# Expert slots of an attention-and-experts kernel: weight planes issued in another order, conversions after the relu, token counts in registers

## Chip, cores and metric

One core of one Trainium2 chip. The metric is the device time of one execution in microseconds (us), the median of the runs shown; smaller is better.

## What is computed

Three layers, one after the other, on 1792 tokens of 768 numbers:

```python
attn = softmax(mask(q @ k.T / 8)) @ v             # 4 x 12 heads, 448 x 64 each
e = argmax(x @ w_gate, axis=1)                    # one of 8 experts per token
for e in range(8):
    h = np.maximum(x[mask] @ w1[e], 0.0)          # 768 -> 1024
    out[mask] = gate * eom * (h @ w2[e])          # 1024 -> 768
h = x @ w_in                                      # 768 -> 2048
y = (h - np.tanh(h)) @ w_out                      # 2048 -> 768
```

## The kernel before

Three stages stand one after the other on the matmul engine (PE): attention, the experts, and the last two matmuls. Every matmul of float32 numbers in the last two stages is made of three float16 matmuls: a number is split into a high plane (the number rounded to float16) and a low plane (the rest), and high x high, high x low and low x high are added. So every weight has to be converted: `scaled` (L110) makes the high plane on ScalarE (ACT), GpSimd (POOL) or VectorE (DVE), and `rest_of` (L118) makes the low plane on DVE or POOL from the float32 number and the high plane.

The change lies in the expert stage. Tokens are sorted by expert into blocks of 128. One block of one expert is a **slot** (`slot`, L812): the matmuls with w1 in two halves of 512 hidden numbers (`slot_mm1`, L157); after each half a relu that writes its high plane hh on ACT and its low plane hl on DVE (`slot_relu`, L164 and L165); the transposition of the token rows of the following slots on PE, copied from PSUM by ACT (high) and DVE (low) (`slot_xT`, L144 to L148); and the matmuls with w2 in two halves of 384 columns (`slot_mm2`, L169), each copied out by ACT into yo (L831) and stored by a DMA (L837).

Every expert has a **first slot**, which always runs, and up to 13 **further slots**, nested in each other, each behind a branch on the expert's token count (`extra`, L847). With these inputs the experts 0 to 7 run 0, 1, 2, 0, 1, 0, 4 and 1 further slots, so 17 slots in all. The count is loaded from SBUF into a register of every engine before each first slot (L1104).

Beside its own matmuls a slot does other work, handed to it as `fill` and called at four positions z = 0 to 3 (after each relu, after each half of w2):

- A first slot of expert e converts the weights of expert e+1 by a table (`PLAN`, L914, and `PLANS` for two experts): for each position some row blocks (0, k) of w1 and (1, k) of w2, with the engine of the high and that of the low plane. `pieces` (L130) issues the high planes of a position, its low planes, and then on the SyncE (SP) queue the loads of expert e+2's rows into the same float32 buffer (L104).
- A further slot converts units of 128 x 1024 numbers of the last stage's weights (`conv`, L876): six DVE instructions (L864, L867, L870) that make float32 of 64-bit words, two ACT instructions for the high plane and two on DVE or four on POOL for the low one. `CPE` gives one to three units per slot, by expert, and `conv_fill` (L890) their positions. Each unit is loaded (L874) and stored again (L885) by SP.

```python
        for fg in range(2):
            ph = slot_mm1(e, i, fg, w, tag)
            slot_relu(fg, ph, hh, hl)
            (fill if late else early)(fg)
```

All engines run their instructions in the order written: nothing is rescheduled. So what stands ahead of a relu on ACT or DVE holds it up, and what stands ahead of a load on SP holds that up. At a branch that is not taken SP and POOL wait for their DMAs under way before they go on (L851).

## Time and profile before

| | |
|---|---|
| device time, median of 3 runs | 1089.51 us (1086.93 to 1093.47) |
| profiled execution: its own time, its span | 1095.17 us, 1093.1 us |
| busy in the span: PE, DVE, POOL, ACT | 1000.8, 830.8, 611.3, 591.9 us |
| mean granted clock of PE | 0.98 |
| expert stage, about 264 to 613 us | 349.2 us, PE busy 302.1 |
| last stage, 613 us to the end | 479.9 us, PE busy 454.2 |

The profile lists each instruction with start and duration, and with the idle time of its engine before it and the event that ended it. An engine that is not busy costs nothing by itself; what counts is idle time of PE, which the other engines feed.

### The profile page before, as it was taken

Reading aid. Unit: us, or ns where it says so; the run is one execution under the profiler, and the core shown is the slowest. Engines: PE = TensorE matmul, PEld = TensorE weight load, DVE = VectorE, ACT = ScalarE, POOL = GpSimd, SP = SyncE. Lnnn points to the kernel's source line nnn. Section 1 sums busy time; section 2 is a strip of 40 time slices with the busy share of each in tenths; the row PEclk is TensorE's granted clock in tenths of the full one; section 3 lists DMA queues with packets and bytes.
Section 4 is the critical chain, followed back from the end, with each engine's and each line's share of the span. In section 5 each row is a group of like instructions: output and inputs, shape, how many; then the busy total and the mean of one; then the engine's idle time right before and its main releaser. Section 6 shows DMA issues by size and latency. Waiting matters only on the chain. (4 is left out here: it accounts for less than half of the span.)

```text
span 1093.1 us, 24262 instructions
## 1 busy us (share of the span) xinstructions
PE 1000.8 (92%) x9186; PEld 749.4 (69%) x9186; DVE 830.8 (76%) x1579; ACT 591.9 (54%) x1190; POOL 611.3 (56%) x623
## 2 busy tenths in 40 slices
PE   5999999998888899789898877999999999999996
PEld 4999998996657667467667544566666666667763
DVE  7778887776896767688785799998788888776640
ACT  4687866773534255263232476666565656655530
POOL 5576765684876348587325867755554444443321
PEclk9999998999999999899999999999999999999998
DMA  8899996735977968984896625010000000000000
GB/s 249 206 252 301 248 273 175 216 99 169 325 256 283 305 233 280 347 273 159 306 315 243 249 115 207 3 42 31 14 24 30 22 27 18 15 16 15 16 23 22
DMA packets 62833, 174.93 MB, mean 160 GB/s; under 512 B 8400, under 2 KB 23376, under 8 KB 59584
## 3 DMA queue, kind: packets, MB, share of 16 engines
q1 hardware_dynamic: 56352, 147.20, 41.1%
q0 software_dynamic: 6304, 25.63, 8.3%
q8 instruction: 80, 1.31, 0.5%
q14 instruction: 97, 0.79, 0.2%
HBM read 133.09 MB, written 29.62 MB: 149 GB/s over the span
## 5 line engine op out<-in xcount | busy, mean ns | idle before, releaser
L1231 PE MATMUL fo<-wo,g 128*128 128x384 f16 x1344 | 228.2, 326 | 0.0
L1180 PEld LDWEIGHTS <-raw 128*128 128x128 f16 x1440 | 141.4, 98 | 95.8 <-issue 18.2
L1231 PEld LDWEIGHTS <-g 128*128 128x128 f16 x1344 | 131.2, 98 | 83.8
L1190 POOL TENSOR_TENSOR V<-cu,cc 128x384 f32<-128x384 f32 (+1 forms) x80 | 77.0, 963 | 197.8 <-ACT cu L1189 197.7
L157 PEld LDWEIGHTS <-w 128*128 128x128 f16 x2592 | 147.8, 99 | 17.4 <-issue 16.4
L169 PE MATMUL py<-w,hh 128*128 128x384 f16 x544 | 137.2, 335 | 18.7 <-ACT hh L164 18.6
L1180 PE MATMUL fh<-cu,raw 128*128 128x384 f16 (+1 forms) x864 | 133.9, 311 | 11.7 <-DVE cc L1188 11.6
L343 ACT ACTIVATE P<-s,nb 112x112 f32<-112x112 f32 (+1 forms) x192 | 90.2, 497 | 62.0 <-DVE nb L337 36.6
L380 PE MATMUL o<-v,PT 112*112 112x65 f32 x960 | 115.9, 261 | 0.0
L120 DVE SCALAR_TENSOR_TENSOR w<-raw,w 128x768 f16<-128x768 f32 (+1 forms) x70 | 99.0, 1455 | 19.0 <-ACT w L112 16.2
L380 PEld LDWEIGHTS o<-v,PT 112*112 112x112 f32 x960 | 106.8, 180 | 0.2 <-ACT xt L402 0.2
L1208 DVE TENSOR_TENSOR V<-V,co 128x384 f32<-128x384 f32 (+1 forms) x80 | 99.9, 1249 | 0.0
L169 PE MATMUL py<-w,hl 128*128 128x384 f16 x272 | 91.1, 335 | 8.0 <-DVE hl L165 7.9
L1189 ACT ACTIVATE cu<-cc 128x384 f32<-128x384 f32 (+1 forms) x80 | 40.1, 502 | 102.5 <-DVE cc L1188 102.5
L1193 POOL TENSOR_TENSOR X<-cc,X 128x384 f32<-128x384 f32 (+1 forms) x80 | 91.0, 1138 | 4.2 <-ACT X L1192 0.5
L1188 DVE TENSOR_TENSOR cc<-fh,co 128x384 f32<-128x384 f32 (+1 forms) x80 | 42.0, 525 | 65.8 <-PE fh L1180 53.9
L169 PEld LDWEIGHTS <-hh 128*128 128x128 f16 x544 | 52.8, 100 | 54.5 <-ACT hh L164 21.9
L329 DVE TENSOR_REDUCE nm<-s 112x2 f32<-112x224 f32 (+1 forms) x144 | 77.2, 536 | 15.7 <-PE s L321 14.2
L128 POOL TENSOR_TENSOR w<-scm,w 128x512 f16<-128x512 f32 (+1 forms) x58 | 77.0, 1327 | 18.6 <-issue 10.9
L1200 DVE SCALAR_TENSOR_TENSOR V<-cu,V 128x384 f32<-128x384 f32 (+1 forms) x80 | 86.7, 1084 | 0.1
L112 ACT ACTIVATE w<-raw 128x768 f16<-128x768 f32 (+2 forms) x101 | 84.1, 892 | 0.0
L157 PE MATMUL ph<-xT_n,w 128*128 128x128 f16 x1152 | 68.4, 222 | 12.2 <-issue 3.5
(430 smaller groups left out, 2049.5 us busy)
## 6 DMA issues: line engine op xcount, KB each, us to landing
raw<-w SPq DMA_DIRECT2D x48, 512.0 KB
raw<-w SPq DMA_DIRECT2D x60, 384.0 KB
cu<-wf SPq DMA_DIRECT2D x22, 1024.0 KB
wb_d<-co SPq DMA_DIRECT2D x22, 512.0 KB
raw<-kq SPq DMA_DIRECT2D x11, 896.0 KB
ys_d<-yo SPq DMA_DIRECT2D x17, 384.0 KB
raw<-wb_d SPq DMA_DIRECT2D x8, 768.0 KB
xs_d<-xq SPq DMA_DIRECT2D x24, 224.0 KB
```

What stands on the lines that cost most here:

```text
L112: nc.scalar.activation(out=out, in_=in_, func=AF.Copy, scale=WS)
L120: nc.vector.scalar_tensor_tensor(out=out, in0=in_, scalar=WS, in1=hi, op0=ALU.mult, op1=ALU.subtract)
L157: nc.tensor.matmul(out=ph[:, (f % 4) * 128 : (f % 4 + 1) * 128], lhsT=w[0][:, ww, k, f * 128 : (f + 1) * 128], rhs=xTs[tag][:, xx, k, :], ...
L169: nc.tensor.matmul(out=py[:, 0:384], lhsT=hx[:, k, :], rhs=w[1][:, ww, k, z * 384 : (z + 1) * 384], start=(k == 0 and n == 0), stop=(k == ...
L329: nc.vector.tensor_reduce(out=nm[:, c0:c1], in_=d["s", m], op=ALU.max, axis=AX.X, negate=True)
L343: nc.scalar.activation(out=d["P"][:, j, OFF[i] : OFF[i] + n], in_=d["s", m][:, z, :], func=AF.Exp, bias=d["nb"][:, 2 * i + j : 2 * i + j + ...
L380: nc.tensor.matmul(out=po[:, i, :], lhsT=d["PT"][:, g, o : o + CP], rhs=d["t"][3][:, hl, j, :], start=(j == 0), stop=(j == i))
L1180: nc.tensor.matmul(out=ph[:, 0:nt], lhsT=wi[ww][:, f // 4, k, f % 4 * 128 : (f % 4 + 1) * 128], rhs=yy[:, k, 0:nt], start=(q == 0), stop=( ...
L1193: nc.gpsimd.tensor_tensor(out=d["X"], in0=d["h"], in1=d["X"], op=ALU.subtract)
L1200: nc.vector.scalar_tensor_tensor(out=d["V"], in0=d[f"S{z}"], scalar=QD[z - 1], in1=d["V"], op0=ALU.add, op1=ALU.mult)
L1208: nc.vector.tensor_tensor(out=d["V"], in0=d["V"], in1=G[g % 2]["rs"][:, 1, 0:nt], op=ALU.mult)
L1231: nc.tensor.matmul(out=po[:, 0:384], lhsT=t[:, x, k, i * 128 : (i + 1) * 128], rhs=wo_[ww][:, k, z * 384 : (z + 1) * 384], start=(k == 0 a ...
```

## The change

The positions of a slot are written out. High planes get five positions of their own, low planes keep four. The high planes of the first table entry are split: its first two go ahead of the w1 matmuls of the slot, the rest behind the first relu. The row transposition goes ahead of the conversions that followed the second relu. Units of the last stage's weights go to the positions 1 and 3 (two per slot) or 1, 2 and 3 (three per slot); position 0 is gone. All eight counts are loaded into registers ahead of expert 0's first slot.

```diff
     def slot(e, i, w, tag, fill=None, trans=(), then=(), late=False):
-        early = (lambda z: None) if late else fill
+        hi, lo = fill if isinstance(fill, tuple) else (lambda z: None, lambda z: None)
         fill = fill if late else (lambda z: None)
...
-        for fg in range(2):
-            ph = slot_mm1(e, i, fg, w, tag)
-            slot_relu(fg, ph, hh, hl)
-            (fill if late else early)(fg)
...
-            py = slot_mm2(e, i, z, w, hh, hl)
-            early(2 + z)
...
+        hi(0)
+        slot_relu(0, slot_mm1(e, i, 0, w, tag), hh, hl)
+        hi(1)
+        lo(0)
+        slot_relu(1, slot_mm1(e, i, 1, w, tag), hh, hl)
+        rows_T(0)
+        fill(1)
+        hi(2)
+        lo(1)
+        py = slot_mm2(e, i, 0, w, hh, hl)
+        hi(3)
+        out_z(0, py)
+        rows_T(1)
+        lo(2)
+        py = slot_mm2(e, i, 1, w, hh, hl)
+        hi(4)
+        lo(3)
+        out_z(1, py)
...
-                if z == (((1,), (0, 2), (1, 2, 3)) if i == 1 + FB[e] else ((1,), (0, 2), (0, 1, 2)))[c - 1][j]:
+                if z == ((1,), (1, 3), (1, 2, 3))[c - 1][j]:
...
+            def fill_hi(z, e=e):
+                plan = PLANS.get(e, PLAN)
+                todo = (plan[0][:2], plan[0][2:])[z] if z < 2 else plan[z - 1]
+                pieces_hi(wts[e + 1], todo)
...
-        cntr = nc.values_load(cnt[0:1, e : e + 1], min_val=0, max_val=NT)
+        if e == 0:
+            cntrs += [nc.values_load(cnt[0:1, x : x + 1], min_val=0, max_val=NT) for x in range(E)]
+        cntr = cntrs[e]
```

`rows_T(z)` is the transposition of a following slot's rows with the gather behind it; `out_z` copies a half of w2's result into yo and then calls `fill(2 + z)`; `fill_lo` calls `pieces` without its high planes.

The order on ACT in the first slot of expert 4 (w_5 are the weights of expert 5, hh the relu, xT and xT_n transposed rows, yo the result). Before:

```order
L164 ACTIVATE hh_0_21138<-ph_0_0_21141 128x512
L112 ACTIVATE w_5_21107<-raw_89 128x1024 x3
L164 ACTIVATE hh_0_21138<-ph_0_1_21228 128x512
L112 ACTIVATE w_5_21107<-raw_89 128x1024 x2
L148 ACTIVATE xT_4488<-pt_I-21315_21316 128x768
L112 ACTIVATE w_5_21108<-raw_90 128x768 x2
L831 ACTIVATE yo_0_21140<-py_0_0_21334 128x384
```

and with the change:

```order
L112 ACTIVATE w_5_21163<-raw_89 128x1024 x2
L168 ACTIVATE hh_0_21180<-ph_0_0_21185 128x512
L112 ACTIVATE w_5_21163<-raw_89 128x1024
L168 ACTIVATE hh_0_21180<-ph_0_1_21270 128x512
L152 ACTIVATE xT_4488<-pt_I-21345_21346 128x768
L112 ACTIVATE w_5_21163<-raw_89 128x1024 x2
L112 ACTIVATE w_5_21164<-raw_90 128x768 x2
L832 ACTIVATE yo_0_21182<-py_0_0_21376 128x384
```

Two high planes moved ahead of the first relu, and the copy of the transposed rows ahead of two others.

The order on DVE in the same slot (hl is the relu's low plane, w_5 low planes but for the one TENSOR_SCALAR). Before:

```order
L165 SCALAR_TENSOR_TENSOR hl_0_21139<-ph_0_0_21141,hh_0_21138 128x512
L120 SCALAR_TENSOR_TENSOR w_5_21107<-raw_89,w_5_21107 128x1024 x2
L165 SCALAR_TENSOR_TENSOR hl_0_21139<-ph_0_1_21228,hh_0_21138 128x512
L120 SCALAR_TENSOR_TENSOR w_5_21107<-raw_89,w_5_21107 128x1024 x2
L146 COPY xT_4488<-pt_I-21324_21325 128x768
L116 TENSOR_SCALAR w_5_21108<-raw_90 128x768
L120 SCALAR_TENSOR_TENSOR w_5_21108<-raw_90,w_5_21108 128x768 x2
L146 COPY xT_n_4486<-pt_I-21381_21382 128x768
L120 SCALAR_TENSOR_TENSOR w_5_21108<-raw_90,w_5_21108 128x768 x4
```

and with the change:

```order
L169 SCALAR_TENSOR_TENSOR hl_0_21181<-ph_0_0_21185,hh_0_21180 128x512
L120 SCALAR_TENSOR_TENSOR w_5_21163<-raw_89,w_5_21163 128x1024 x2
L169 SCALAR_TENSOR_TENSOR hl_0_21181<-ph_0_1_21270,hh_0_21180 128x512
L150 COPY xT_4488<-pt_I-21354_21355 128x768
L120 SCALAR_TENSOR_TENSOR w_5_21163<-raw_89,w_5_21163 128x1024 x2
L116 TENSOR_SCALAR w_5_21164<-raw_90 128x768
L150 COPY xT_n_4486<-pt_I-21414_21415 128x768
L120 SCALAR_TENSOR_TENSOR w_5_21164<-raw_90,w_5_21164 128x768 x6
```

Both copies of transposed rows moved up by two low planes each.

The order on ACT in the further slot of expert 4, with two units (co are the converted units). Before:

```order
L164 ACTIVATE hh_1_21462<-ph_1_0_21465 128x512
L112 ACTIVATE co_4888<-cc 128x512 x2
L164 ACTIVATE hh_1_21462<-ph_1_1_21572 128x512
L148 ACTIVATE xT_4487<-pt_I-21647_21648 128x768
L831 ACTIVATE yo_1_21464<-py_1_0_21666 128x384
L112 ACTIVATE co_4889<-cc 128x512 x2
L831 ACTIVATE yo_1_21464<-py_1_1_21724 128x384
```

and with the change:

```order
L168 ACTIVATE hh_1_21504<-ph_1_0_21507 128x512
L168 ACTIVATE hh_1_21504<-ph_1_1_21582 128x512
L152 ACTIVATE xT_4487<-pt_I-21657_21658 128x768
L112 ACTIVATE co_4986<-cc 128x512 x2
L832 ACTIVATE yo_1_21506<-py_1_0_21708 128x384
L832 ACTIVATE yo_1_21506<-py_1_1_21734 128x384
L112 ACTIVATE co_4987<-cc 128x512 x2
```

The first unit moved from between the relus to behind both and behind the copy of the rows; the second from ahead of the second result to behind it, where the next slot's first relu follows.

## Rows read from the trace of the kernel before

**Rows 1.** Experts, last stage: length, busy PE, PEld, DVE, ACT, POOL (us), clock, DMA share, GB/s.
```profile
264.00:613.20 349.20, 302.08 (x3571) 234.91 (x3569) 264.40 (x371) 145.39 (x221) 210.42 (x190) 0.97 0.79 275
613.20:1093.10 479.90, 454.20 (x2966) 284.72 (x2966) 366.64 (x602) 269.25 (x545) 235.90 (x224) 0.99 0.12 44
```

**Rows 2.** Waits of PE in the expert stage: us in total, times, longest.
```profile
PE py L169 <- ACT hh L164: 18.6, 9, 5.0
PE py L169 <- DVE hl L165: 7.9, 14, 1.5
...
PE pt_I-25681_25682 L144 <- DVE xT L146: 1.4, 1, 1.4
...
PE pt_I-21381_21382 L144 <- DVE xT L146: 0.6, 1, 0.6
```

**Rows 3.** PE in time, further slots: the longest waits for the second relu.
```profile
446.60 0.82 PE L169 MATMUL py<-w,hh 128*128 128x384 f16 x2 [4.98 <-ACT hh L164]
...
529.95 0.50 PE L169 MATMUL py<-w,hh 128*128 128x384 f16 x2 [4.15 <-ACT hh L164]
```

**Rows 4.** ACT in time, expert 4's further slot, at the 4.98 us wait.
```profile
443.93 0.63 ACT L112 ACTIVATE co<-cc 128x512 f16<-128x512 f32 x1 [6.68 <-DVE cc L870]
...
445.96 0.58 ACT L164 ACTIVATE hh<-ph 128x512 f16<-128x512 f32 x1
```

**Rows 5.** Stretches behind that wait: busy of five engines, granted clock, DMA share, GB/s.
```profile
446.50:449.00 2.50, 1.40 (x4) 0.42 (x5) 2.50 (x5) 0.74 (x2) 2.26 (x3) 0.50 0.89 313
449.00:452.00 3.00, 3.00 (x11) 1.46 (x10) 3.00 (x6) 0.16 (x1) 0.47 (x1) 0.50 0.98 337
```

**Rows 6.** DVE instructions on a unit: ns min/median/max, first and last start.
```profile
L870 DVE SCALAR_TENSOR_TENSOR cc<-cu,cc x44: 675/683/1640, 316.3 to 596.4; 128x512 uint32<-128x512 uint32 x44
```

**Rows 7.** DVE and SP in time: a unit's load issued, and the conversion that waited for it.
```profile
367.40 0.36 SPq L874 DMA_DIRECT2D cu<-wf  x1
...
378.33 0.76 DVE L864 TENSOR_SCALAR cc<-cu 128x512 uint32<-128x512 uint32 x2 [2.28 <-DMA cu<-wf]
```

**Rows 8.** Stretch of expert 6's second further slot, three units.
```profile
514.00:534.00 20.00, 14.87 (x181) 11.40 (x181) 17.42 (x32) 6.04 (x12) 4.87 (x5) 0.93 0.94 335
```

**Rows 9.** PE and DVE in time, expert 3's first slot: start, second transposition.
```profile
391.98 8.21 PE L157 MATMUL ph<-xT_n,w 128*128 128x128 f16 x144 [1.04 <-ACTq L851]
...
406.32 0.49 PE L144 MATMUL pt_I-17081_17082<-identh,xg_n 128*128 128x128 f16 x6 [1.23 <-DVE xT L146]
...
402.25 3.55 DVE L120 SCALAR_TENSOR_TENSOR w<-raw,w 128x1024 f16<-128x1024 f32 x2
405.72 0.55 DVE L146 COPY xT<-pt_I-17024_17025 128x768 f16<-128x768 f16 x1
```

**Rows 10.** POOL and ACT in time, first slots of experts 3 and 4.
```profile
397.93 1.16 POOL L128 TENSOR_TENSOR w<-scm,w 128x512 f16<-128x512 f32 x1 [5.02 <-issue]
...
431.53 0.49 ACT L831 ACTIVATE yo<-py 128x384 f32<-128x384 f32 x1 [6.72 <-SPq L851]
```

**Rows 11.** The loads of the counts on PE and DVE: ns min/median/max, first and last start.
```profile
L1104 PEldq TENSOR_LOAD <-cnt x8: 301/310/497, 261.6 to 574.6; - x8
...
L1104 DVEq TENSOR_LOAD <-cnt x8: 300/330/1623, 273.2 to 584.2; - x8
```

**Rows 12.** Page: low planes on DVE. Then DVE and PE in experts 0 and 1.
```profile
L120 DVE SCALAR_TENSOR_TENSOR w<-raw,w 128x768 f16<-128x768 f32 (+1 forms) x70 | 99.0, 1455 | 19.0 <-ACT w L112 16.2
...
274.16 0.69 DVE L165 SCALAR_TENSOR_TENSOR hl<-ph,hh 128x512 f16<-128x512 f32 x1 [0.80 <-DVE flg L762]
...
306.58 0.71 PE L1038 MATMUL order<-cc,co 112*128 112x70 bf16 x16 [1.22 <-DVE cc L1019]
```

**Rows 13.** PE and ACT in time, from expert 6's last slot into expert 7's first.
```profile
575.16 8.30 PE L157 MATMUL ph<-xT_n,w 128*128 128x128 f16 x144 [1.72 <-DVE cc L867]
...
585.63 1.09 ACT L164 ACTIVATE hh<-ph 128x512 f16<-128x512 f32 x2 [7.95 <-PE pt_I-34952_34953 L144]
586.28 0.50 PE L169 MATMUL py<-w,hh 128*128 128x384 f16 x2 [2.15 <-ACT hh L164]
```

More of the change, by code (lines that the diff above doesn't have):

```diff
@@ L128, in rest_of, with pieces_hi, pieces @@
                 nc.gpsimd.tensor_tensor(out=out[:, c], in0=t, in1=hi[:, c], op=ALU.subtract)
-    def pieces(w, plan, nxt=None):
+    def pieces_hi(w, plan):
         for x, k, eh, el in plan:
             scaled(eh, w[x][:, 0, k, :], (raw1, raw2)[x][:, k, :])
+    def pieces(w, plan, nxt=None, hi=True):
+        if hi:
+            pieces_hi(w, plan)
         for x, k, eh, el in plan:
@@ L817, in slot, with rows_T @@
         yo = mt.tile([128, DM], F32, tag="yo", name=f"yo_{e}_{i}")
-        for fg in range(2):
-            ph = slot_mm1(e, i, fg, w, tag)
-            slot_relu(fg, ph, hh, hl)
-            (fill if late else early)(fg)
         trans = list(trans)
-        for z in range(2):
+        def rows_T(z):
             if trans:
@@ L828, in slot, with out_z @@
                     then[z]()
-            py = slot_mm2(e, i, z, w, hh, hl)
-            early(2 + z)
+        def out_z(z, py):
             nc.scalar.activation(out=yo[:, z * 384 : (z + 1) * 384], in_=py[:, 0:384], func=AF.Copy)
             fill(2 + z)
+        hi(0)
[16 more added lines that the diff above has]
+        out_z(1, py)
         j = i - FB[e]
@@ L1056, in remaining @@
                 remaining(o - 2)
+    cntrs = []
     for e in range(E):
@@ L1068, in build, with fill_lo @@
                 wts[e + 1] = w_tiles(e + 1)
-            def fill(z, e=e):
+            def fill_hi(z, e=e):
+                plan = PLANS.get(e, PLAN)
+                todo = (plan[0][:2], plan[0][2:])[z] if z < 2 else plan[z - 1]
+                pieces_hi(wts[e + 1], todo)
+            def fill_lo(z, e=e):
                 if e == 0 and z >= 2:
                     next(tl, None)
-                pieces(wts[e + 1], PLANS.get(e, PLAN)[z], e + 2)
+                pieces(wts[e + 1], PLANS.get(e, PLAN)[z], e + 2, False)
                 if e == 1 and z > 1:
                     order_a(z) if z < 3 else order_b()
+            fill = (fill_hi, fill_lo)
         else:
```

## Prediction

> **What bounds the kernel now.** I read four views in this order: busy time by stretch, the list of what PE waits for, the order in time on PE, ACT and DVE around the largest of these waits, and the loads and stores beside them.
>
> The stretches tell where the change can act [rows 1]. The expert stage lasts 349.2 us with PE busy for 302.1 of them; DVE, ACT and POOL are busy for 264, 145 and 210. So PE bounds the stage, and up to 47 us of it are idle time of PE. The last stage (479.9 us) runs the same code before and after and starts when the experts end, so what the experts gain or lose moves the end by as much.
>
> The list of waits [rows 2] says what PE's idle time is. Nine times w2's first matmuls wait for the relu's high plane hh, 18.6 us in all, and fourteen times for its low plane hl, 7.9 us. Taken apart by slot (the same list, in time), these 26.5 us are: 15.5 in the five further slots with two units (one of expert 1, two of expert 2, one each of experts 4 and 7), 7.9 in expert 6's four further slots with three units, 2.4 at the start of expert 7, and 0.7 in the first slots of experts 4 and 6. Apart from these, PE waits five times, in the first slots of experts 2 to 6, for DVE's copy of transposed rows, 0.6 to 1.4 us each and 5.0 in all [rows 2].
>
> The cause stands in the order on ACT [rows 3, 4]. In expert 4's further slot the second relu writes hh at 445.96, and PE, which waited 4.98 us for it, goes on at 446.60. Just ahead of the relu ACT stands on the high planes of a unit: it waited 6.68 us for DVE to make the float32 numbers, until 443.93. ACT works in order, so the relu's input lay ready behind a conversion that nobody needed yet. The same holds in expert 6, with 4.15 us [rows 3].
>
> **(a) Two-unit slots.** The first unit moves behind the second relu and the rows' copy, so neither hh nor hl has a unit ahead of it: 15.5 us of waits lose their cause. Behind the longest of them the granted clock is 0.50, the 1.2 GHz level, after PE had idled, until 452 [rows 5]; PE is busy 1.40 + 3.00 = 4.4 us there, which at full clock are 2.2. Upper end 17.7. In such a slot PE may still wait a moment for hl, some 0.23 us, as at the smallest of these waits: 5 x 0.23 = 1.2 off. I take **+16.5**. What hides the unit now is the time of w2's two halves, some 8 us; DVE has eight instructions on a unit there, none longer in the median than 683 ns [rows 6], so up to 5.5 us a unit and 11 in a slot of 17. If that cover is gone (late loads, or DVE behind from a first slot, as in expert 4's), the relu of the next slot waits instead; half of the gain is the lower end, 8.
>
> **(b) Expert 6's four slots.** 7.9 us of waits, and 1.0 for the clock: 0.93 over 14.87 busy us in the second of them [rows 8]. But there DVE is busy 17.42 of 20.0 us and the DMA share is 0.94, near the 0.98 of the fullest stretch [rows 5]. A unit's load needs 378.33 - 367.40 = 10.9 us in such a crowd, and DVE waited 2.28 for that one [rows 7]. Four slots cannot shrink far below 17.4 us each while DVE has that much to do, nor much past a few per cent while the transfers are the same. I take **+4**, between 0 and 8.9.
>
> **(c) Rows' copies in first slots.** In expert 3 DVE makes two low planes for 3.55 us from 402.25, only then copies the rows at 405.72, and the second transposition on PE waits 1.23 [rows 9]. With the copy ahead of them this goes in all five first slots: 5.0 us, and 0.7 for hl's waits there. What is late next: the same low planes, and the transposed rows of the next expert behind the same copies. I take **+5**, between 3 and 5.7.
>
> **(d) Experts 0 and 1.** Here DVE is the chain: it has hl of the first relu at 274.16, and PE waits 1.22 for cc from DVE at 306.58 [rows 12]. Seven more count loads stand on DVE before expert 0's first relu, at a median of 330 ns 2.3 us [rows 11]; the low planes' waits for ACT's high planes (16.2 us over the whole kernel [rows 12]), of which I count 1.1 in these two experts, mostly go, as the first two high planes are earlier. The expected loss is 2.3 - 1.1, and 0.3 that the reordered copies bring at the order matmul: **-1.5**. Bounds: -3.5 (seven loads at the longest load of PE, 497 ns [rows 11], nothing regained) and +1.8 (expert 1's transposition also waits 1.80 for such a copy, by the same list).
>
> **(e) Counts.** On PE a load takes 310 ns in the median [rows 11] and lies in the idle time before a first slot, as in the 1.04 us at 391.98 [rows 9]. Seven go: 7 x 0.31 = **+2.2** (0 if the branch's other instructions or ACT fill the gap, 3.5 at 497 ns each). The seven that PE gains at expert 0 start at 261.6, beside matmuls still running; without that cover they cost the same 2.2. Against this stands the Trainium skill, page "DMA: Bandwidth & Descriptors", section "Latency and other measured facts": it gives `tensor_load` a floor of some 600 ns. By that, an estimate, (e) would be +4.2 and DVE's part of (d) 4.2 instead of 2.3, the sum nearly the same; the trace does not agree (310 and 330 ns), and the trace decides.
>
> **(f) Entry of expert 7.** Expert 6's last slot has its third unit late on DVE already: PE's start there waits 1.72 for a conversion, and the hh at 586.28 waits 2.15, ACT having stood behind the transposition [rows 13]. With PE earlier and the same work behind it this grows: **-1**, between 0 and -3 (a third again of the two waits, and nearly the double).
>
> **(g) New waits.** Two high planes ahead of the first relu on ACT, units at a slot's end ahead of the next slot's relu, and pairs of first slots in which POOL and the merge on SP bound the end: yo of expert 4 waited 6.72 for SP's branch [rows 10]. POOL can start sooner, as it idled 5.02 before 397.93 [rows 10]. SP's queue has the unit's store and next load later by the same move; with some 17 us until the next use and 10.9 until landing [rows 7] this costs nothing, unless the transfers slow further. No row prices it whole: between 0 and -6 (nearest row: the 6.72 again). I take **-2.5**, nearer to nothing, as PE still has 4 us of w1's first half (half of 8.21 [rows 9]) before the relu in question is due.
>
> **Sum.** 16.5 + 4 + 5 - 1.5 + 2.2 - 1 - 2.5 = 22.7 us. The profiled execution's 1095.17 becomes 1072.5; the median lies 5.66 below the profiled one, so it becomes 1089.51 - 22.7 = 1066.8, **1067**. All terms at their good ends give 37.6 (1052), all at their bad ends -1.5 (1091).
>
> **Rivals.**
>
> *The first slots and expert 6 are bound by DVE, POOL and DMA.* Then (b) and (c) give nothing, since the freed time is idled again a little later: 16.5 - 1.5 + 2.2 - 1 - 2.5 = 13.7, **1076**. For it: the DMA share of 0.94 [rows 8], and that DVE's instruction on a unit takes up to 1640 ns against 683 in the median [rows 6]. Against it: over the stage DVE is idle for 85 us of 349, POOL for 139 [rows 1]. By the Trainium skill, page "SBUF — State Buffer", section "Who interferes with whom", a DVE instruction with two SBUF inputs contends with a GpSimd instruction that reads SBUF; that would work for this rival, since POOL starts sooner beside the low planes on DVE. The row with 1640 agrees, but does not show which engine held it up.
>
> *The units' own work, not their place, is what is late.* Then half of (a) comes back as waits for the next relu, and (b) and (c) are nothing: 8 - 1.5 + 2.2 - 1 - 2.5 = 5.2, **1084**. The change then doesn't do what it says. For it: ACT waited 6.68 for DVE [rows 4], which stays so. Against it: hh's input was ready all that time.
>
> *Slower: the unit at a slot's end holds up the next slot's first relu.* Nine further slots end with a unit on ACT ahead of the next relu. It decides from the point where that conversion ends over 4.1 us into the next slot. To eat the 22.7 and 7 more, each of the nine must hold PE up by 3.3 us: 9 x 3.3 = 29.7, **1097**. For it: PE reaches the next slot sooner, while DVE, loads and POOL stay as they are, and in expert 6 a clock drop might follow each wait. Against it: the unit's load is late by 2.28 us in the row shown [rows 7], which would leave nearly half of the 4.1.
>
> **Chances.** The forecast 0.66, since the cause of its main term stands in an order that the change alters; the first rival 0.18, the second 0.09, the slower one 0.07. A measurement of this kernel can tell about 0.5% from no change, 5.4 us: faster is below 1084.1, slower above 1095.0. Faster takes the forecast, nearly all of the first rival and half of the second, 0.86; slower most of the third, 0.06; the same, 0.08. The range of 1056 to 1081 holds the forecast with its unknown terms at either side and the first rival; about 0.17 lies outside, the second and third rival and the good ends all at once.
>
> **What would show it.** Right: the hh and hl waits of experts 1, 2 and 4 gone from PE's list; no wait for DVE's copy in experts 2 to 6; a granted clock of 1.00 in expert 4's further slot; an expert stage of some 326 us; the last stage still 480. (d) is right if PE's wait at the order matmul grows by about 1.5, (f) if expert 7's hh waits 3 instead of 2.15. The first rival shows as equally long slots in expert 6 with DVE or DMA full, the second as ACT waiting for DVE with a relu behind it, the third as PE waits for hh at the first relu of the slots that follow a further slot. The prediction is wrong if the stage gains less than 14 us or more than 33.

## The result, and the profile after

The changed kernel takes 1075.28 us, the median of 4 runs (1074.73 to 1077.59), beside 1089.51 for the kernel before in the same comparison. The ratio is 0.987, with a 95% interval of 0.9835 to 0.9904: some 14 us less, where 22.7 were forecast. The time lies in the range of 1056 to 1081, 8 us above the 1067 named, and close to the 1076 of the first rival. Repeated beside other kernels, the change took 1079.12 us (1075.02 to 1087.33), ratio 0.990 (0.9853 to 0.9947). Three executions in a slower state of the chip are in no median: 1178.84 us of the kernel before here, and 1098.05 and 1489.19 us of two kernels below.

Busy time in two stretches of the profile after, experts and last stage (columns as in [rows 1]):

```profile
260.80:593.40 332.60, 298.32 (x3568) 236.29 (x3568) 256.48 (x371) 145.75 (x221) 207.60 (x190) 0.98 0.81 287
593.40:1073.50 480.10, 454.24 (x2966) 285.13 (x2966) 365.15 (x601) 268.76 (x544) 235.44 (x224) 0.99 0.13 46
```

The expert stage is 16.5 us shorter, 332.6 against 349.1 from the first matmul of expert 0 (264.70 before, 260.85 after) to the first of the last stage; the last stage has its length of before. The profiled spans differ by 19.6 us, but 3.9 of it lies ahead of expert 0, and in all the profiles of this case that start lies anywhere between 258.5 and 268.0. So I compare lengths of slots, each from PE's first w1 matmul to that of the next slot. This leaves out one thing that the change does ahead of expert 0: PE's pause for the eight loads of counts there, 0.76 us in this profile and 2.29 in the repetition, and none before.

What PE waits for in the expert stage after:

```profile
PE py L173 <- DVE hl L169: 11.4, 13, 2.6
PE py L173 <- ACT hh L168: 9.2, 6, 4.5
PE order L1058 <- DVE cc L1039: 2.9, 1, 2.9
```

Against [rows 2], the waits for hh are half (18.6 before), those for hl have *grown* (7.9 before), and the five waits for DVE's copy of transposed rows are gone. Lengths in us, summed by kind of slot; the last column is a kernel whose slots run the code of before (the run "The counts alone" below):

| slots | before | change | change, repeated | counts alone |
|---|---|---|---|---|
| four further slots with two units (experts 1, 2, 4) | 89.2 | 71.2 | 72.9 | 86.9 |
| four further slots with three units (expert 6) | 79.5 | 72.0 | 75.8 | 76.6 |
| first slots of experts 0 to 6 | 141.8 | 146.2 | 139.4 | 143.9 |
| first slot of expert 7 | 19.3 | 24.3 | 26.7 | 16.9 |
| further slot of expert 7 | 19.3 | 19.0 | 18.4 | 22.1 |
| all | 349.1 | 332.6 | 333.3 | 346.4 |

Each column is one execution. The first and the last run the same code in the slots, and so do the two of the change, and yet they differ by up to 2.9 and 6.8 us in a row; so a difference of a few us in one row need not be an effect. The two-unit slots and expert 7's first slot differ by more than that.

The further slots gained 25.8 us and the first slots gave 9.3 of it back; in the repetition 20.9 (with expert 7's) and 5.1, where experts 5 and 7 lost 1.6 and 7.4 and the other first slots gained. The further slots first. Expert 4's and the second three-unit slot of expert 6, as stretches:

```profile
415.45:434.65 19.20, 16.85 (x207) 13.24 (x204) 15.52 (x19) 9.15 (x15) 17.17 (x16) 1.00 0.88 310
...
495.98:514.50 18.52, 16.85 (x205) 13.32 (x204) 16.05 (x30) 6.21 (x12) 4.88 (x6) 1.00 0.93 323
```

They were 27.3 and 24.0 us long; the granted clock, 0.50 behind the long wait [rows 5], is 1.00 throughout (in the repetition expert 4's took 21.8 us at 0.92, with a wait of 2.53 for hl). Now the first slots. PE in time, experts 3, 5 and 7:

```profile
376.71 8.21 PE L161 MATMUL ph<-xT_n,w 128*128 128x128 f16 x144 [0.63 <-ACT yo L832]
...
391.37 0.34 PE L173 MATMUL py<-w,hl 128*128 128x384 f16 x1 [2.62 <-DVE hl L169]
...
434.65 8.21 PE L161 MATMUL ph<-xT_n,w 128*128 128x128 f16 x144 [0.67 <-ACT yo L832]
...
446.50 0.50 PE L173 MATMUL py<-w,hh 128*128 128x384 f16 x2 [1.76 <-ACT hh L168]
...
451.05 0.34 PE L173 MATMUL py<-w,hl 128*128 128x384 f16 x1 [1.71 <-DVE hl L169]
...
564.68 0.80 PE L173 MATMUL py<-w,hh 128*128 128x384 f16 x2 [4.51 <-ACT hh L168]
```

In expert 5 PE starts at 434.65, so the first relu's input is ready 4.1 us later, at 438.8. ACT and DVE in time there:

```profile
436.83 1.23 ACT L112 ACTIVATE co<-cc 128x512 f16<-128x512 f32 x2 [2.33 <-DVE cc L890]
443.95 2.00 ACT L112 ACTIVATE w<-raw 128x1024 f16<-128x1024 f32 x2 [5.89 <-ACTq L871]
445.86 0.58 ACT L168 ACTIVATE hh<-ph 128x512 f16<-128x512 f32 x1
```

```profile
437.49 1.29 DVE L120 SCALAR_TENSOR_TENSOR co<-cc,co 128x512 f16<-128x512 f32 x2
446.47 0.69 DVE L169 SCALAR_TENSOR_TENSOR hl<-ph,hh 128x512 f16<-128x512 f32 x1 [7.69 <-ACT hh L168]
447.08 3.31 DVE L120 SCALAR_TENSOR_TENSOR w<-raw,w 128x1024 f16<-128x1024 f32 x2
450.32 0.68 DVE L169 SCALAR_TENSOR_TENSOR hl<-ph,hh 128x512 f16<-128x512 f32 x1
```

The relu comes at 445.86, 7 us late. Ahead of it ACT and DVE end the second unit of expert 4's further slot and then take the branch out of the nest of further slots. The rows of that branch (L871) on DVE, ahead of expert 3 and ahead of expert 5, and on ACT ahead of expert 5 (ns, then first and last start):

```profile
L871 DVEq COMPARE_BRANCH  x2: 47/64/80, 377.8 to 385.2; - x2
L871 DVEq EVENT_SEMAPHORE  x1: 21/21/21, 385.1 to 385.1; - x1
```

```profile
L871 DVEq COMPARE_BRANCH  x2: 47/60/74, 438.1 to 444.3; - x2
L871 DVEq EVENT_SEMAPHORE  x1: 21/21/21, 444.2 to 444.2; - x1
```

```profile
L871 ACTq COMPARE_BRANCH  x2: 38/48/59, 437.4 to 443.6; - x2
L871 ACTq EVENT_SEMAPHORE  x1: 17/17/17, 443.5 to 443.5; - x1
```

DVE is at the branch at 438.1 and lets others see that it has left it at 444.2, 6.1 us later; ACT needs 437.4 to 443.5. The same rows before, on DVE and ACT ahead of expert 5, where PE started at 457.28:

```profile
L851 DVEq COMPARE_BRANCH  x2: 54/67/80, 453.4 to 459.7; - x2
L851 DVEq EVENT_SEMAPHORE  x1: 21/21/21, 459.6 to 459.6; - x1
```

```profile
L851 ACTq COMPARE_BRANCH  x2: 43/51/59, 456.2 to 461.2; - x2
L851 ACTq EVENT_SEMAPHORE  x1: 17/17/17, 461.1 to 461.1; - x1
```

The branch took as long, but both engines reached it *before* PE began the new expert, and left it 2.3 and 3.8 us after that start, in time for a relu due at 4.1. Now they leave it 9.5 and 8.9 us after. In the profile after, the first relus of experts 1 to 6 start at 7.8, 8.4, 8.5, 6.4, 11.2 and 9.2 us of their slots; before, at 6.5, 8.6, 4.3, 5.3, 4.6 and 5.2. Four of them (experts 1, 3, 4 and 6) start some 0.1 us after DVE's event, as here in expert 3, where DVE's event ended at 385.13:

```profile
385.25 0.60 ACT L168 ACTIVATE hh<-ph 128x512 f16<-128x512 f32 x1 [2.34 <-DVEq L871]
```

Expert 2's waited for PE's own matmuls and is no later than before. Expert 5's comes 1.7 us after DVE's event: ACT, which had left the branch itself only at 443.5, first makes the two high planes (443.95 to 445.95 in the rows above). So in that expert the high planes put ahead of the relu do cost time, behind a late branch.

What a late relu costs depends on how late it is. PE needs hh only after w1's second half and the rows' transposition: at 6.4 us (expert 4) PE has no such wait in the slot, at 8.5 it waits 0.20 for hh (expert 3), at 11.2 1.76 (expert 5), at 13.8 4.51 (expert 7).

### The profile page after: what moved, and what is told of

The parts are those of the page before. It is cut to its first block, busy times and chain, and to the rows that moved or that the text cites. A ratio compares the mean times of both kernels' runs of the same rounds, so it can differ in the third digit from the quotient of the medians.

```text
span 1073.5 us, 24251 instructions
## 1 busy us (share of the span) xinstructions
PE 994.7 (93%) x9186; PEld 748.5 (70%) x9186; DVE 821.6 (77%) x1579; ACT 592.8 (55%) x1190; POOL 607.5 (57%) x623
## 5 line engine op out<-in xcount | busy, mean ns | idle before, releaser
L161 PEld LDWEIGHTS <-w 128*128 128x128 f16 x2592 | 150.1, 100 | 13.4 <-issue 12.3
L173 PE MATMUL py<-w,hh 128*128 128x384 f16 x544 | 133.8, 328 | 9.3 <-ACT hh L168 9.2
L128 POOL TENSOR_TENSOR w<-scm,w 128x512 f16<-128x512 f32 (+1 forms) x58 | 81.4, 1403 | 11.5 <-issue 6.2
L1230 DVE SCALAR_TENSOR_TENSOR V<-cu,V 128x384 f32<-128x384 f32 (+1 forms) x80 | 86.8, 1085 | 0.1
L173 PEld LDWEIGHTS <-hh 128*128 128x128 f16 x544 | 52.2, 98 | 42.0 <-ACT hh L168 10.5
```

Of the source, the lines that this page charges most:

```text
L128: nc.gpsimd.tensor_tensor(out=out[:, c], in0=t, in1=hi[:, c], op=ALU.subtract)
L161: nc.tensor.matmul(out=ph[:, (f % 4) * 128 : (f % 4 + 1) * 128], lhsT=w[0][:, ww, k, f * 128 : (f + 1) * 128], rhs=xTs[tag][:, xx, k, :], ...
L173: nc.tensor.matmul(out=py[:, 0:384], lhsT=hx[:, k, :], rhs=w[1][:, ww, k, z * 384 : (z + 1) * 384], start=(k == 0 and n == 0), stop=(k == ...
L1230: nc.vector.scalar_tensor_tensor(out=d["V"], in0=d[f"S{z}"], scalar=QD[z - 1], in1=d["V"], op0=ALU.add, op1=ALU.mult)
```

## The experiments

**Theory 1, the late branch**: what the change puts behind the second relu ends later against PE; ACT and DVE come later to the branch, need 4 to 7 us for it, and the next expert's first relu is late. **Theory 2**: the two high planes put ahead of the first relu hold it up.

**The further slots alone.** The kernel before, with the order of the change in the further slots (`late`), and in expert 7's first slot, which is built as they are:

```diff
+        if not late:
...
+        else:
+            slot_relu(0, slot_mm1(e, i, 0, w, tag), hh, hl)
+            slot_relu(1, slot_mm1(e, i, 1, w, tag), hh, hl)
...
-                if z == (((1,), (0, 2), (1, 2, 3)) if i == 1 + FB[e] else ((1,), (0, 2), (0, 1, 2)))[c - 1][j]:
+                if z == ((1,), (1, 3), (1, 2, 3))[c - 1][j]:
```

> The kernel before with the change's further slots alone (units behind the second relu, at positions 1 and 3 or 1, 2 and 3); first slots and count loads as before. Theory 1, the late branch: a unit that begins behind the second relu ends later against PE, so DVE and ACT come later to the branch at the expert's end, leave it 4 to 7 us after that, and the next first slot's first relu is late. Further slots then shorten by about 25 us in all, as in the change, and first slots lengthen by 7 to 11 us: about 1075. Theory 2, the high planes ahead of the first relu: they wait for the weights' loads and hold the relu up; without them the first slots keep their lengths of before, and the time is about 1066.

Measured: 1079.36 us, ratio 0.990 (0.9856 to 0.9939). Further slots 25.1 us shorter (expert 7's included), first slots 13.9 us longer (175.0 against 161.1), 10.0 of it in experts 0 to 6, whose first slots run the code of before: theory 1's signs. Theory 2's 1066 did not come, and the loss is there without its cause. ACT in expert 5's first slot, where PE started at 435.99 and no high plane stands ahead of the relu:

```profile
438.31 1.23 ACT L112 ACTIVATE co<-cc 128x512 f16<-128x512 f32 x2 [2.84 <-DVE cc L886]
446.37 0.60 ACT L164 ACTIVATE hh<-ph 128x512 f16<-128x512 f32 x1 [6.82 <-DVEq L867]
```

10.4 us after PE's start, released by DVE's event (L867 is the branch there).

**The first slots alone.** The change, with the further slots' order, their positions and the count loads of before:

```diff
+        if late:
+            for fg in range(2):
+                ph = slot_mm1(e, i, fg, w, tag)
+                slot_relu(fg, ph, hh, hl)
+                fill(fg)
...
-                if z == ((1,), (1, 3), (1, 2, 3))[c - 1][j]:
+                if z == (((1,), (0, 2), (1, 2, 3)) if i == 1 + FB[e] else ((1,), (0, 2), (0, 1, 2)))[c - 1][j]:
...
+        cntr = nc.values_load(cnt[0:1, e : e + 1], min_val=0, max_val=NT)
```

> The change's first slots alone (high planes ahead of the first relu, rows' copies ahead of the conversions); further slots and count loads as before. Theory 1: the branches come as early as before, the five waits for DVE's copy of rows go, about 5 us: about 1085, and the first relu of the first slots of experts 3 and 5 starts within 5 us of PE's start. Theory 2: the first slots lengthen as in the change, by 9 us or more, and the rows' copies give 5 back at most: 1094 or more.

Measured: 1090.39 us, ratio 0.998 (0.9946 to 1.0021), not to be told from no change. The first slots did shorten by 5.5 us (155.6), and did not lengthen by theory 2's 9. The first relu of expert 3 starts 4.3 us into its slot, as before; that of expert 5 at 6.8, not within theory 1's 5: ACT left the branch 4.1 us in and then made the two high planes, so theory 2 has a share there, with a wait of 0.85 us for hl behind it. The time that theory 1 gave, 1085, was missed too. The further slots got 4.3 us longer, but 3.1 of it lies in expert 7's, which is 2.8 longer in the run with the counts alone as well; whether the gain came back as waits cannot be told from this profile.

**The counts alone.**

```diff
-        cntr = nc.values_load(cnt[0:1, e : e + 1], min_val=0, max_val=NT)
+        if e == 0:
+            cntrs += [nc.values_load(cnt[0:1, x : x + 1], min_val=0, max_val=NT) for x in range(E)]
+        cntr = cntrs[e]
```

> The kernel before with all counts loaded at expert 0 and nothing else. Both theories: PE's pause ahead of the first slots of experts 2 to 6 falls from 0.8 to 1.1 us to 0.4 to 0.7, some 2 to 3 us in all, and DVE's seven loads cost up to 2.3 us at experts 0 and 1: between 1086 and 1091, not to be told from no change by the time alone; the pauses tell.

Measured: 1089.76 us, ratio 0.998 (0.9956 to 0.9999). PE's pause ahead of expert 3's first slot, 1.04 us before [rows 9]:

```profile
387.19 8.21 PE L157 MATMUL ph<-xT_n,w 128*128 128x128 f16 x144 [0.70 <-ACTq L851]
```

The seven pauses add up to 4.5 us instead of 7.4, 2.9 us less, each by 0.34 to 0.51. But ahead of expert 0, where it went on without a pause before (at 264.70), PE now pauses too:

```profile
263.05 1.11 PE L157 MATMUL ph<-xT_n,w 128*128 128x128 f16 x17 [2.25 <-issue]
```

The loads start 0.40 to 0.43 us apart there, from 259.67 to 262.12, and the matmuls under which they began had ended 2.25 us before PE goes on. So of the 2.9 us some 0.7 is left.

The three parts one by one take 11.1, 1.9 and 2.4 us off by these ratios, 15 together; the whole takes 14. The interval of the second holds no change and that of the third all but touches it. So the further slots carry the change.

**DVE's words earlier.** If the late branch is the cost, a unit that begins earlier on DVE, without standing ahead of a relu on ACT, should get it back. The change, with the six DVE instructions of the first unit's `to_f32` (part 1 of `conv`) at position 0:

```diff
+        fill(0)
         hi(1)
         lo(0)
...
+                if z == 0 and j == 0:
+                    conv(cu[b], None, None, part=1)
                 if z == ((1,), (1, 3), (1, 2, 3))[c - 1][j]:
```

> The change, but DVE makes the float32 words of a further slot's first unit behind the first relu, as before; ACT's high planes and the low planes stay behind the second relu. Theory 1: DVE comes to the branch some 3 us earlier than in the change, and the first slots behind further slots (experts 2, 3, 5 and 7) regain 2 to 4 us each while the further slots keep what they gained: 1065 to 1069. Theory 2: nothing ahead of the first relu of a first slot is different, so 1075 as the change.

Measured: 1082.24 us, ratio 0.990 (0.9881 to 0.9925), not the 1065 to 1069 of theory 1. The first slots did come back, 160.3 us against 170.4 (166.2 in the repetition), as the theory wants; but the four two-unit slots went from 71.2 (72.9) to 83.9. DVE and then PE in expert 4's further slot:

```profile
429.58 0.68 DVE L169 SCALAR_TENSOR_TENSOR hl<-ph,hh 128x512 f16<-128x512 f32 x1
430.19 1.53 DVE L885 TENSOR_SCALAR cc<-cu 128x512 uint32<-128x512 uint32 x2
431.63 2.43 DVE L888 SCALAR_TENSOR_TENSOR cc<-cu,cc 128x512 uint32<-128x512 uint32 x2
433.99 1.75 DVE L891 SCALAR_TENSOR_TENSOR cc<-cu,cc 128x512 uint32<-128x512 uint32 x2
435.67 0.68 DVE L169 SCALAR_TENSOR_TENSOR hl<-ph,hh 128x512 f16<-128x512 f32 x1
...
437.93 0.75 DVE L885 TENSOR_SCALAR cc<-cu 128x512 uint32<-128x512 uint32 x2
438.60 1.28 DVE L888 SCALAR_TENSOR_TENSOR cc<-cu,cc 128x512 uint32<-128x512 uint32 x2
```

```profile
430.32 0.34 PE L173 MATMUL py<-w,hl 128*128 128x384 f16 x1 [2.65 <-DVE hl L169]
...
436.40 0.50 PE L173 MATMUL py<-w,hl 128*128 128x384 f16 x1 [2.74 <-DVE hl L169]
```

Low planes of the first slot hold DVE until 429.7; then the words come between the two hl and take 5.5 us, with POOL still at its planes until 434.6, where the next unit's, with POOL idle, take 0.75 and 1.28 a pair. PE waits 2.65 and 2.74 us, and its clock falls: 0.82 granted over the slot. So in this slot DVE's work on the unit delays the second half as well, not ACT's order alone.

**High planes behind the first relu.**

```diff
-        hi(0)
         slot_relu(0, slot_mm1(e, i, 0, w, tag), hh, hl)
+        hi(0)
         hi(1)
```

> The change, but with all high planes of a first slot's first table entry behind the first relu, as before. Theory 1, the late branch: in the change the first relu of experts 1 to 6 starts within 0.1 us after DVE has left the branch, so the two high planes ahead of it cost nothing there; the first relu of the first slots still starts 7 to 10 us after PE where a further slot came before, and the time stays at 1073 to 1078. Theory 2, the high planes hold the relu up: the first slots regain most of the 9 us that they lost, 1066 to 1069.

Measured: 1081.96 us, ratio 0.991 (0.9883 to 0.9936). The first relus of experts 1 to 6 still start 6.1 to 8.6 us into their slots, the first slots take 168.7 us in all (170.4 and 166.2 in the change), and the time is not 6 us below that of the change: theory 2 does not account for the loss. The premise of theory 1, that the two high planes cost nothing in the change, does not hold for expert 5: its relu now starts 7.8 us into the slot, 0.1 behind DVE's event, where the change had 11.2 and 9.5. In expert 5 (PE from 445.81) ACT reads:

```profile
453.64 0.60 ACT L168 ACTIVATE hh<-ph 128x512 f16<-128x512 f32 x1 [6.04 <-DVEq L871]
```

**Low planes later; units' low planes on POOL; both.** One line each:

```diff
         hi(1)
-        lo(0)
         slot_relu(1, slot_mm1(e, i, 1, w, tag), hh, hl)
...
+        lo(0)
         lo(1)
```

> The change, but a first slot's first low planes come behind the second relu and the rows' copy instead of between the two relus. In the change PE waits 1.7, 2.6, 1.7 and 0.9 us for hl of the second relu in the first slots of experts 1, 3, 5 and 6, with some 4 us of low planes ahead of it on DVE. Theory 1: after a late first relu both relus come at once, and these low planes then stand in the way: the four waits go, 4 to 7 us: 1069 to 1072. Rival: DVE's end is what sets the next slot, and low planes begun later only move the lateness to the next branch: 1075 or more, with DVE leaving the branch later than in the change.

```diff
-                    conv(cu[b], co[b][:, 0], co[b][:, 1], "p" if j == 2 else "v")
+                    conv(cu[b], co[b][:, 0], co[b][:, 1], "p" if j or c == 2 else "v")
```

> The change, but the low planes of a further slot's units are made by POOL: both of two, the second and third of three. DVE then has 1.3 us less per unit behind the relus. Theory 1: DVE leaves the branch ahead of experts 2, 3, 5 and 7 1.3 to 2.6 us earlier, and the first relus there start earlier by as much: 1068 to 1072. Theory 2 sees nothing changed: 1075. A third outcome: POOL, with four instructions per unit of some 4 us in all, slows DVE or holds its own branch, and the time is 1076 or more.

> The change with both: first low planes behind the second relu, and low planes of units on POOL. Theory 1: the gains add, 1064 to 1069, as the earlier branch also makes up for low planes begun later. If the rival of the first holds, no better than the low planes on POOL alone.

Measured: 1091.4 us, ratio 0.999 (0.9961 to 1.0019), with low planes later; 1099.9, 1.007 (1.0036 to 1.0102), with POOL; 1105.46, 1.013 (1.0091 to 1.0164), with both. All three expectations of theory 1 failed. With low planes later its rival holds: DVE leaves the branch ahead of experts 4 and 6 10.2 and 9.9 us after PE's start instead of 6.3 and 9.1 (7.1 and 7.9 in the repetition), and expert 1's order matmul now waits 7.3:

```profile
PE order L1058 <- DVE cc L1039: 7.3, 1, 7.3
```

With POOL the third outcome holds. The stage's busy times:

```profile
264.30:618.40 354.10, 307.74 (x3569) 238.67 (x3570) 246.95 (x345) 145.19 (x221) 251.31 (x238) 0.95 0.77 271
```

DVE has 9.5 us less to do than in the change and POOL 43.7 more, and the stage takes 21.5 more. POOL holds the unit's float32 words for longer, so the next unit begins later on DVE, which waited 2.3 us in all for this in the change:

```profile
DVE cc L884 <- POOL scm L114: 15.6, 11, 2.4
```

The unit then ends later on ACT, which reaches the branch ahead of experts 2, 3 and 5 4.0, 5.9 and 5.1 us after PE's start (0.9, 0.4 and 2.8 in the change).

**Words earlier, only where DVE carries nothing over.** Beside it the change again, and the same kernel with position 2 for 3:

```diff
+                late1 = i > 1 + FB[e]
+                if z == 0 and j == 0 and late1:
+                    conv(cu[b], None, None, part=1)
```

```diff
-                if z == ((1,), (1, 3), (1, 2, 3))[c - 1][j]:
+                if z == ((1,), (1, 2), (1, 2, 3))[c - 1][j]:
```

> The changed kernel itself, once more, beside the other two on one chip. Both theories: 1073 to 1078, and in its profile the first slots again longer than before by 5 us or more in all, those behind further slots above all, and the first relu of experts 1 to 6 again within 0.1 us of the moment at which DVE left the branch.

> The change, with the first unit's float32 words made by DVE behind the first relu, but only from an expert's second further slot on, where DVE carries nothing over from a first slot. Theory 1: the further slots right behind a first slot stay as in the change; those of experts 2 and 6 that follow lose nothing, DVE comes to the branch ahead of experts 3 and 7 some 2 to 3 us earlier, and their first relus start earlier by as much: 1067 to 1072. Against theory 1: 1075 or more, or unchanged starts of these two relus.

> As the one before, but in slots with two units the second unit is ahead of the second result on ACT and ahead of the result's store on SP (position 2 instead of 3). DVE's order is the same. Theory 1: DVE's end sets the branch, so the time is that of the one before within 3 us. If ACT's or SP's own order at the slot's end counted, the first slots of experts 2, 3 and 5 would change by 2 us or more each.

Measured: 1079.12, 1079.06 and 1082.87 us, ratios 0.990 (0.9853 to 0.9947), 0.990 (0.9856 to 0.9936) and 0.993 (0.9894 to 0.9968). In the repeated change the first relus of experts 1, 4 and 6 came 0.1 us after DVE's event, as expected, those of experts 2, 3 and 5 0.7 to 1.4 us after it; its time was a little above the 1073 to 1078, and its first slots 5.1 us longer than before, those of experts 2 and 3 shorter. With the words earlier, expert 7's first relu came 10.3 us into its slot (10.8 in the third kernel) instead of 13.8 and 15.0, and that slot took 19.6 us (19.9) instead of 24.3 and 26.7: half of the expectation is met. The other half failed: DVE reached the branch ahead of expert 3 1.0 us after PE's start, as in the change (1.1 and 1.1), and the relu there came at 7.3 (8.5 and 6.2). And the whole is no faster. Two-unit slots took 78.0, three-unit slots 77.8, and expert 7's further slot 22.2 instead of 19.0, so both slots of expert 7 together took 41.8 us instead of 43.3 and 45.2, with 38.6 before. PE in expert 6's second further slot:

```profile
508.15 0.50 PE L173 MATMUL py<-w,hh 128*128 128x384 f16 x2 [1.18 <-ACT hh L168]
...
513.72 0.50 PE L173 MATMUL py<-w,hl 128*128 128x384 f16 x1 [2.72 <-DVE hl L169]
```

The expectation against theory 1, "1075 or more", is met. Moving the second unit ahead of the result is 3.8 us slower by the medians, more than the 3 that were expected and within the noise of this pair; the first slots of experts 2, 3 and 5 changed by 1.8, 1.1 and 0.4 us, less than the 2 each that would have shown ACT's or SP's own order at the slot's end.

How the earlier words reach expert 7 is in the rows of expert 6's last slot. Its third unit goes into the buffer that its first unit leaves, so the third unit's load stands on SP behind the first unit's words. SP and DVE before (PE at expert 7: 575.16), then in the change (550.20), then with the words earlier (557.00):

```profile
565.89 0.34 SPq L874 DMA_DIRECT2D cu<-wf  x1
573.40 0.77 DVE L864 TENSOR_SCALAR cc<-cu 128x512 uint32<-128x512 uint32 x2 [0.65 <-DMA cu<-wf]
```

```profile
545.46 0.33 SPq L894 DMA_DIRECT2D cu<-wf  x1
553.49 0.76 DVE L884 TENSOR_SCALAR cc<-cu 128x512 uint32<-128x512 uint32 x2 [2.01 <-DMA cu<-wf]
```

```profile
549.82 0.33 SPq L895 DMA_DIRECT2D cu<-wf  x1
557.41 0.76 DVE L885 TENSOR_SCALAR cc<-cu 128x512 uint32<-128x512 uint32 x2 [1.28 <-DMA cu<-wf]
```

The load takes 7 to 8 us each time. Against PE's start of expert 7 it is issued 9.3 us ahead before, 4.7 in the change (2.9 repeated) and 7.2 with the words earlier, and DVE begins on the unit 1.8 us ahead, 3.3 (4.8) and 0.4 us after. So what was late ahead of expert 7 was a load, and DVE's work behind it.

**Less work for DVE, none for POOL.**

```diff
-        [(1, 2, "a", "p"), (1, 0, "v", "v"), (1, 1, "a", "v")],
+        [(1, 2, "a", "p"), (1, 0, "a", "v"), (1, 1, "a", "v")],
```

> The change, but the one high plane per first slot that DVE makes (experts 2 to 6, some 0.5 to 1.5 us each) goes to ACT. Theory 1 in the form that the runs leave (DVE's end sets the branch and the next relu, and DVE beside POOL is what the stage has least of): DVE comes to the branch 0.5 to 1.5 us earlier ahead of experts 4 and 6, and hl of the first further slots of experts 4 and 6 is less late; 3 to 6 us off the change: 1071 to 1076 where the change has 1075 to 1079. If PE's waits only change places, as with the words made earlier, within 2 us of the change.

Measured: 1075.4 us, ratio 0.987 (0.9831 to 0.9911): the change's. DVE is busy 4.2 us less, the stage takes 332.5 us. DVE leaves the branch ahead of expert 4 4.4 us into the slot instead of 6.3, but the first relu there starts at 6.9 instead of 6.4, behind the two high planes, which ACT begins only when it has left the branch itself, 4.7 us in; expert 6's starts at 9.7 instead of 9.2. The waits for hl in the first further slots of these experts are 1.54 and 1.52 us, in the change 1.68 and 1.06. PE's waits only changed places. None of the kernels tried beats the change by more than can be measured.

## Why the prediction was right or wrong

The direction and the main term were right, and the range held; the sum was 8 us too good, chiefly because the entry of expert 7 was priced too low, and because the loads of the counts cost at expert 0 most of what they give back later. That the time fell within the range owes something to luck: in the first profile (b) gave nearly twice its forecast, and the repetition's 1079.12 left 2 us to the upper end.

- **(a), right.** +16.5 was forecast; the four two-unit slots gained 18.0 and, repeated, 16.3, of which the shorter pauses ahead of experts 2, 3 and 5 are 1.3. In expert 4's the clock stayed at 1.00, as said (0.92 repeated), but a wait for hl of 1.68 and 2.53 us is left there. One part was misread: expert 7's further slot converts no unit. Its two units are in its *first* slot, so its waits (1.44 and 0.23) had no place in the 15.5, and 1.13 and 0.23 of them are still there.
- **(b), right within its bounds.** +4 was forecast; 7.5 and 3.7 came. DVE is busy 16.05 of 18.52 us with the DMA share at 0.93 in the slot shown.
- **(c), right as a wait, not shown as a gain.** All five waits for the rows' copy went. In the run with the first slots alone experts 2 to 6 gave 5.5 us; in the whole change the same slots wait for hl instead, 2.62 in expert 3 and 1.71 in expert 5: the relus come so late that both fall together, and low planes stand between their two hl.
- **(d), right as a wait.** The order matmul waits 2.86 instead of 1.22 (forecast: 1.5 more), 2.3 in the repetition. The first slots of experts 0 and 1 together took 0.2 us more and 1.0 less, not 1.5 more.
- **(e), right in its first half, wrong in its second.** +2.2 was forecast; alone it took 2.9 off the pauses. By the 600 ns that the Trainium skill, page "DMA: Bandwidth & Descriptors", section "Latency and other measured facts", gives, it would have been 4.2 by an estimate; the runs are nearer to the row's 310 ns. What failed is the cover at expert 0: "beside matmuls still running" held for the first loads only, and PE paused 2.25 us there in the run with the counts alone, 0.76 and 2.29 in the change. The prediction had named this condition and taken it as met.
- **(f), the step that failed.** It was -1, at worst -3: expert 7's first slot lost 4.9 and 7.4. The sum had this entry grow by a third, and (g) said of the later loads on SP that "with some 17 us until the next use" they cost nothing. In a slot of three units the next use is the third unit of the same slot: the load is issued 4.5 us later against PE, and DVE begins 5.1 us later on that unit. Behind it stand two branches one after the other, the nest's and a second one (L1069, for weights that no slot has converted), and the relu comes at 13.8 instead of 10.5:

```profile
564.03 1.08 ACT L168 ACTIVATE hh<-ph 128x512 f16<-128x512 f32 x2 [6.65 <-ACTq L1069]
```

- **(g), the right place, its size open.** It was -2.5, "nearer to nothing, as PE still has 4 us of w1's first half ... before the relu in question is due". With this, (c), (d) and the three pauses of (e) that lie in them, the first slots of experts 0 to 6 should have gained 1.9 us; they lost 4.4, and gained 2.3 in the repetition. The comparison with 4 us left out that at an expert's end DVE needs 4 to 7 us for the branch *after* its last instruction, and that the relu also waits for DVE's event. The trace of before had the row (453.4 to 459.6 on DVE); I read the unit's own end and not the branch behind it. In both profiles this cost expert 5 time, 3.8 and 1.6 us; in the others the two profiles disagree.

The first rival's 1076 was met, but not as it was told: (b) came, and (c)'s waits went. Its open question, what held up the instruction of 1640 ns [rows 6], the traces answer: POOL was at work beside it (see the end). The slower rival named the right place, a unit at a slot's end ahead of the next slot's first relu. In expert 6's further slots that relu is late too (6.4 to 9.7 us in), but PE waits for hh in one of them only, 1.44 us; the price fell on the first slots of the experts that follow a further slot, 5 and 7 above all. The second rival was right in one thing: DVE's work on the unit can be late by itself, as in the run with all words earlier.

What stays open is why gains in one kind of slot came back as waits in the other. Words earlier gave the first slots 10 and 13 us against the first profile of the change and took 20 and 16 from the further ones (6 and 9, and 15 and 11, against the repetition). DVE with 4 us less to do gave nothing. A hint is in the sum of neighbours: expert 4's further slot took 19.2, 21.8, 23.2 and 17.7 us in the change, its repetition, the run with words earlier from the second further slot on and the further slots alone, and together with expert 5's first slot 43.0, 43.4, 42.7 and 43.3. So time moves between the two, and one profile of one slot tells little. That DVE, beside POOL, is what this stage has least of would fit this, but the run that loaded POOL with 43.7 us more also made DVE wait for POOL's reads, and no run had DVE markedly relieved without burdening POOL; the units' loads, for which DVE waits 4.1 and 8.6 us in the two profiles of the change, are a rival that no run tested. So it is argued and not shown. A buffer for hh of the first slots' own, so that the relu need not wait for DVE's event, was not tried.

## What to carry to other kernels

Work that is taken from ahead of a wait is put somewhere, and its new end is what must be priced: add what the engine has behind its last instruction, here 4 to 7 us of branch on DVE, and compare that with the next time PE needs the engine. A load that waits for a buffer moves with the work that empties the buffer, and its next use may be nearer than the next round. An idle engine by the stage's mean (DVE 85 us of 349) may have none left in the slots that matter; look at the stretch, and at what it carries over from the one before. Compare sums over neighbouring slots, and two executions of the same code, before a difference in one slot is called an effect. Try each part of a change alone: here one of three carried it.

## What the runs showed of the hardware that was not expected

- The branch out of the nest takes an engine long: from its compare to its event DVE needed 4.0 to 7.3 us ahead of experts 2 to 7 in the two profiles, ACT 0.5 to 6.1, PE 3.1 each time. PE pauses for 0.4 to 1.8 us only ahead of these experts' first slots, as its sequencer is ahead of its matmuls; on ACT and DVE the time shows in full. What an engine does in it, no row says.
- A load of a number into a register of PE took 301/310/497 ns (least, median and most of 8) [rows 11], and seven in a row started 0.40 to 0.43 us apart; where no matmul was left to cover them, PE stood still for 2.25 us.
- DVE's instructions on the words slowed down beside POOL's work. In the trace of before, 34 of those at L867 ran while POOL computed nothing, and none took more than 0.70 us; of the 8 that had POOL at work for most of their time the median took 1.09 and the longest 1.65. Those at L864, with one input from SBUF, went the same way: a median of 0.42 us for 30 without POOL, 0.72 for 12 with it. Some beside POOL were not slowed, and which of POOL's instructions does it was not looked into.
